# A six-layer cross network on one core: one remainder transposed by VectorE, one group of products moved, one load cut into twelve

## The chip, the cores and the metric

The kernel runs on one NeuronCore of one Trainium2 chip. The metric is the device time of one execution in microseconds (us), as the median of several runs. In what follows PE is TensorE's matmul side and PEld its weight load, DVE is VectorE, ACT is ScalarE, POOL is GpSimd and SP is SyncE; a "q" behind a name (SPq, ACTq) is the part of that engine that issues DMAs and waits.

## The reference

The inputs are x0 of 4096 rows by 416 columns, six weight matrices of 416 by 416 and six biases of 416, all bf16. Six times the current x is multiplied by a matrix, a bias is added, the sum is multiplied element by element by x0, and x is added.

```python
B, F, D, L = 4096, 26, 16, 6
def reference(x0, ws, bs):
    x = x0
    for l in range(ws.shape[0]):
        x = x0 * (x @ ws[l] + bs[l]) + x
    return x
```

## The kernel before

**Layout.** x is kept transposed, with features on the 128 partitions and rows of x0 along the free axis. 416 features are three blocks of 128 (k and m run over them) and a remainder of 32. The three blocks lie in XM: XM[0] holds x0, XM[1] and XM[2] are used in turn for the later layers. The remainder lies in XR in the same way, packed: the 4096 rows are two halves (s = 0, 1) of four column groups of 512 (g = 0 to 3), and the 32 remainder features of group g lie on partitions 32g to 32g+31. XRd is a copy of x0's remainder with the two halves of the partitions exchanged, used by one block of the first layer (m = 1).

**How x0 gets there.** The three blocks come by eight transposing loads on SP's queue (load_x0t, L75), four to a half. The remainder can't come that way. For the first half, four loads on ACT's queue (load_xrem0, L80) bring 64-byte pieces of rows into xrig, four PE transposes (x0_rem, L155) write them to PSUM, and three DVE copies (L158) fill XR[0] and XRd. For the second half, one load on SP's queue (load_xrem1, L84), placed between the transposing loads of that half, fills xrem, a POOL copy (L132) rearranges it into xrig, and x0_rem then does with it as with the first: four PE transposes into half of the PSUM tile pr, and three DVE copies.

**First layer** (first_layer, once for each half). Full products (L212, 128x128 weights, 512 columns), remainder rows (row, L219: 32 partitions of weights, four groups side by side in the array), and products that make the remainder features (mm_rem, L191 and L196: 32 columns of weights, four groups side by side). The outputs of three m and a half-half h lie in PSUM tiles of two banks each; there are four such tiles in all, so a new one waits until ACT has read an old one. ACT adds the bias and moves each tile to SBUF (L163), DVE multiplies by x0 (L164) and adds x (L167). The remainder takes the same way through L171, L172 and L173. For the first half, the call of x0_rem for the second half stands after mm_rem and before the elementwise work of h = 1.

**Layers two to five** (the loop over l from 1). The work is six blocks (s, m), taken in pairs: n = 0, 2, 4 is the first block of a pair. A block is 48 products in column tiles (L179) and four row products (L185). Behind the first pair (n = 0) comes rem_pair: the remainder products of both halves (8 of L191 and 24 of L196) into one PSUM tile, then two ACT and four DVE operations that fill the next XR.

**Last layer.** Rows of the output are made directly, 128 at a time: full products (L325), remainder (L331) and bias (L334), then ACT (L352) and two DVE operations (L353, L342) that multiply by X0rows and add XLrows. X0rows holds x0 by rows and is loaded by four DMAs on SP's queue (L123), behind all weights; bLr (L125) follows. XLrows is x after layer five, put back to rows by transposing DMAs on SP's queue (L203).

**Order.** The order of instructions on each engine follows the program, with a scheduler that may move DVE and ACT work among neighbours; what is handed to keep_in_program_order stays as written. Each engine works its own list in order. DMAs are issued in order on each queue, and a DMA semaphore that is used again makes the issue wait for its earlier user.

Of the kernel before, what the change touches and what calls it, by code (L numbers as in the profile page):

```python
# [11 lines left out]
BF16 = mybir.dt.bfloat16  # L12
# [4 lines left out]
def kernel(  # L17
# [7 lines left out]
    nc = tc.nc  # L25
    B, D = x0.shape
    L = ws.shape[0]
    P = 128
    NK = 3
    R = D - NK * P  # L30
    assert R == 32 and B == 4096 and D == 416 and L >= 2
    NS = 2
    NG = 4
    CW = 512
    SW = NG * CW
    NBT = B // P
# [3 lines left out]
    big = ctx.enter_context(tc.tile_pool(name="big", bufs=1))  # L40
# [4 lines left out]
    x0_v = x0.rearrange("(bt p) d -> p bt d", p=P)  # L45
    out_v = out.rearrange("(bt p) d -> p bt d", p=P)

    ident = const.tile([P, P], BF16)
# [9 lines left out]
    X0rows = big.tile([P, NBT, D], BF16)  # L58
    XLrows = big.tile([P, NBT, D], BF16)
    scrR = [big.tile([P, 4, P], BF16, name=f"scrR{s}") for s in range(NS)]  # L60
    xrem = big.tile([P, 16, R], BF16)
    xrig = big.tile([P, NS, 4, P], BF16)
    XRd = big.tile([P, NS * CW], BF16)
    XM = [big.tile([P, NK, B], BF16, name=f"XM{i}") for i in range(3)]
    XR = [big.tile([P, NS * CW], BF16, name=f"XR{i}") for i in range(3)]

    def col0(s, g):
        return SW * s + CW * g

    def load_wm(eng, l):  # L70
        eng.dma_start(WM[:, l], ws[l, 0:NK * P, :].rearrange("(k p) n -> p k n", p=P))

    def load_x0t(s, g):
        c0 = col0(s, g)
        nc.sync.dma_start_transpose(out=XM[0][:, :, c0:c0 + CW], in_=x0[c0:c0 + CW, 0:NK * P])  # L75

    def load_xrem0():
        with nc.allow_non_contiguous_dma(reason="64B row segments"):
            for i in range(4):
                nc.scalar.dma_start(xrig[:, 0, i, :].rearrange("p (g r) -> p g r", g=NG), x0_v[:, i:16:4, NK * P:D])  # L80

    def load_xrem1():
        with nc.allow_non_contiguous_dma(reason="64B row segments"):
            nc.sync.dma_start(xrem[:], x0_v[:, 16:32, NK * P:D])  # L84

    def load_wr0():
        nc.scalar.dma_start(WR[0:R, 0, :], ws[0, NK * P:D, :])
# [17 lines left out]
    for g in range(1, NG):  # L105
        dst, src = WR[32 * g:32 * g + 32, 0, :], WR[0:R, 0, :]
# [4 lines left out]
    for g in range(2, NG):  # L111
        load_x0t(0, g)
    load_x0t(1, 0)
    load_xrem1()
    for g in range(1, NG):
        load_x0t(1, g)
    load_wm(nc.sync, 1)
# [1 line left out]
        load_wr(nc.sync, g, 1, L)  # L119
    for l in range(2, L):  # L120
        load_wm(nc.sync, l)
    for q in range(4):
        nc.sync.dma_start(X0rows[:, 8 * q:8 * q + 8, :], x0_v[:, 8 * q:8 * q + 8, :])  # L123
    for g in range(NG):
        nc.sync.dma_start(bLr[32 * g:32 * g + 1, :], bs[LL:LL + 1, :])  # L125

    def fill_wd(l0, l1):
        for g in range(NG):
            nc.gpsimd.tensor_copy(WD[32 * g:32 * g + 32, l0:l1, g, :], WR[32 * g:32 * g + 32, l0:l1, NK * P:D])

    fill_wd(0, 1)
    nc.gpsimd.tensor_copy(xrig[:, 1].rearrange("p i (g r) -> p i g r", g=NG), xrem[:].rearrange("p (g i) r -> p i g r", g=NG))  # L132
    fill_wd(1, L)

    wps = psum.tile([P, CW], FP32, tag="ps", name="wps")
# [14 lines left out]
        nc.vector.tensor_copy(bM[:], pb[:, 0:NK, 0:L])  # L150
        nc.vector.tensor_copy(bR[:], pb[:, 3, 0:L])

    def x0_rem(s, tpr):
        for i in range(4):
            nc.tensor.transpose(tpr[:, 128 * i:128 * i + 128], xrig[:, s, i, :], ident[:])  # L155
        for dst, src in ((slice(0, P), slice(0, P)), (slice(64, P), slice(0, 64)), (slice(0, 64), slice(64, P))):
            to = XR[0] if dst == src else XRd
            nc.vector.tensor_copy(to[dst, CW * s:CW * s + CW], tpr[src])  # L158

    def ew_main(l, s, m, h, pt, cur, nxt, pin=False):  # L160
        c0 = col0(s, 2 * h)
        t = tpool.tile([P, 2 * CW], BF16, name="t")
        nc.scalar.activation(t[:], pt[:].rearrange("p a b -> p (a b)"), ACT.Identity, bias=bM[:, m, l:l + 1], scale=1.0)  # L163
        prod = nc.vector.tensor_tensor(out=t[:], in0=t[:], in1=XM[0][:, m, c0:c0 + 2 * CW], op=ALU.mult)  # L164
        if pin:
            tc.keep_in_program_order(prod)
        nc.vector.tensor_tensor(out=nxt[:, m, c0:c0 + 2 * CW], in0=t[:], in1=cur[:, m, c0:c0 + 2 * CW], op=ALU.add)  # L167
# [21 lines left out]
    def mm_rem(l, s, pr, cur, curR):  # L189
        for g in range(NG):  # L190
            nc.tensor.matmul(pr[32 * g:32 * g + 32, :], lhsT=WD[:, l, g, :], rhs=curR[:, CW * s:CW * s + CW],  # L191
                             start=True, stop=False, tile_position=(0, 32 * g))
        for k in range(NK):
            for g in range(NG):
                c0 = col0(s, g)
                nc.tensor.matmul(pr[32 * g:32 * g + 32, :], lhsT=WM[:, l, k, NK * P:D], rhs=cur[:, k, c0:c0 + CW],  # L196
                      start=False, stop=(k == NK - 1), tile_position=(0, 32 * g))

    def new_pts():
        return [psum.tile([P, 2, CW], FP32, tag="ps", name=f"pt{h}") for h in range(2)]  # L200

    def xl_dmat(s, k, nxt):
        nc.sync.dma_start_transpose(out=XLrows[:, 16 * s:16 * s + 16, 128 * k:128 * k + 128],  # L203
                                    in_=nxt[:, k, SW * s:SW * s + SW])

    def first_layer(s):
        cur, curR, nxt, nxtR = XM[0], XR[0], XM[1], XR[1]

        def full(pt, m, h, gl, after_row):
            c0 = col0(s, 2 * h + gl)  # L210
            for k in range(NK):
                nc.tensor.matmul(pt[:, gl, :], lhsT=WM[:, 0, k, 128 * m:128 * m + 128], rhs=cur[:, k, c0:c0 + CW],  # L212
                                 start=(k == 0 and not after_row), stop=(k == NK - 1 and after_row))

        def row(pt, m, h, opens):
            for gl in range(2):
                rg = 32 * ((2 * h + gl) ^ (2 if m == 1 else 0))
                src = XRd if m == 1 else curR
                nc.tensor.matmul(pt[:, gl, :], lhsT=WR[rg:rg + 32, 0, 128 * m:128 * m + 128],  # L219
                                 rhs=src[rg:rg + 32, CW * s:CW * s + CW],  # L220
                                 start=opens, stop=not opens, tile_position=(rg, 0))

        def ph(m):
            return psum.tile([P, 2, CW], FP32, tag="ps", name=f"ph{m}")

        pa = [ph(m) for m in range(NK)]
        if s == 0:
            for m in range(NK):
                full(pa[m], m, 0, 0, False)
            tp0 = psum.tile([P, CW], BF16, tag="ps", name="tpr")  # L230
            x0_rem(0, tp0[:])
            for m in range(NK):
                full(pa[m], m, 0, 1, False)
        else:
            for m in range(NK):
                for gl in range(2):
                    full(pa[m], m, 0, gl, False)
        pb = [ph(0)]
        row(pa[0], 0, 0, False)
        row(pb[0], 0, 1, True)  # L240
        row(pa[2], 2, 0, False)
        row(pa[1], 1, 0, False)
        for m in range(NK):
            ew_main(0, s, m, 0, pa[m], cur, nxt)
        for m in range(NK):
            if m:
                pb.append(ph(m))
            for gl in range(2):
                full(pb[m], m, 1, gl, m == 0)
        row(pb[1], 1, 1, False)  # L250
        row(pb[2], 2, 1, False)
        pr = psum.tile([P, 2, CW], FP32, tag="ps", name="pr")
        mm_rem(0, s, pr[:, 0, :], cur, curR)
        if s == 0:
            x0_rem(1, pr[:, 1, :].bitcast(BF16)[:, 0:CW])
        for m in range(NK):
            ew_main(0, s, m, 1, pb[m], cur, nxt, pin=(s == 0))
        ew_rem(0, s, pr[:, 0, :], curR, nxtR)
# [3 lines left out]
    for s in range(NS):  # L262
        first_layer(s)
# [16 lines left out]
    for l in range(1, LL):  # L280
        nxt, nxtR = XM[1 + (l % 2)], XR[1 + (l % 2)]
        feeds_last = (l == LL - 1)
        tiles = [(s, m) for s in range(NS) for m in range(NK)]
        pts = {}

        def finish(t):
            s, m = t
            for h in range(2):
                ew_main(l, s, m, h, pts[t][h], cur, nxt)
            if feeds_last:  # L290
                xl_dmat(s, m, nxt)

        for n in range(0, len(tiles), 2):
            ta, tb = tiles[n], tiles[n + 1]
            pts[ta] = new_pts()
            for g in range(NG):
                mm_full(l, ta[0], ta[1], g, pts[ta], cur, True, False)
            mm_row(l, ta[0], ta[1], pts[ta], curR, False, True)
            pts[tb] = new_pts()
            mm_row(l, tb[0], tb[1], pts[tb], curR, True, False)  # L300
            if feeds_last and n == 4:
                xl_rem(0)
            finish(ta)
            for g in range(NG):
                mm_full(l, tb[0], tb[1], g, pts[tb], cur, False, True)
            finish(tb)
            if n == 0:
                rem_pair(l, cur, curR, nxtR, feeds_last)
        if feeds_last:
            xl_rem(1)  # L310
        cur, curR = nxt, nxtR

    l = LL
# [97 lines left out]
```

## Time and profile before

| what | value |
|---|---|
| median of 3 runs | 130.45 us (130.38 to 130.53) |
| profiled execution | 130.58 us |
| span of that execution, first to last instruction | 128.8 us |
| granted TensorE clock, mean | 1.000 |
| PE busy | 123.6 us (96%), 1691 matmuls |
| DVE busy | 106.7 us (83%) |
| ACT busy | 86.9 us (67%) |
| POOL busy | 6.2 us (5%) |
| DMA | 16.37 MB |

The span is shorter than the time by what lies before the first and after the last instruction. The groups that the change touches:

```profile
L191 PE MATMUL pr<-XR,WD 128*32 128x512 bf16 x40 | 3.9, 381 | 0.0
L132 POOL COPY xrig<-xrem 128x512 bf16<-128x512 bf16 x1 | 1.1, 1057 | 3.7 <-DMA xrem<-in_x_dram 3.7
L158 DVE COPY XRd<-pr 64x512 bf16<-64x512 bf16 x2 | 0.8, 422 | 0.0
L158 DVE COPY XR<-pr 128x512 bf16<-128x512 bf16 x1 | 0.4, 425 | 0.5 <-PE pr L155 0.5
L155 PE MATMUL pr<-ident,xrig 128*128 128x128 bf16 x4 | 0.4, 222 | 0.0
```

Each line is a group: source line, engine, operation, output and inputs with their shapes, the number of instructions, then the busy time in us and the mean of one in ns, and behind the second bar the idle time of the engine just before them and what ended it. Matmuls are pipelined: a mean of 381 ns does not mean that PE was held that long by each. The time that a group holds PE is read from the chain of waits.

### The profile page before, as it was taken

Reading aid. Unit: us, or ns where it says so; the run is one execution under the profiler, and the core shown is the slowest. Engines: PE = TensorE matmul, PEld = TensorE weight load, DVE = VectorE, ACT = ScalarE, POOL = GpSimd, SP = SyncE. Lnnn points to the kernel's source line nnn. Section 1 sums busy time; section 2 is a strip of 40 time slices with the busy share of each in tenths; the row PEclk is TensorE's granted clock in tenths of the full one; section 3 lists DMA queues with packets and bytes.
Section 4 is the critical chain, followed back from the end, with each engine's and each line's share of the span. In section 5 each row is a group of like instructions: output and inputs, shape, how many; then the busy total and the mean of one; then the engine's idle time right before and its main releaser. Section 6 shows DMA issues by size and latency. Waiting matters only on the chain.

```text
span 128.8 us, 3973 instructions
## 1 busy us (share of the span) xinstructions
PE 123.6 (96%) x1691; PEld 55.1 (43%) x1691; DVE 106.7 (83%) x195; ACT 86.9 (67%) x99; POOL 6.2 (5%) x18
## 2 busy tenths in 40 slices
PE   7999999999999999999999999999999999999960
PEld 3343443344545444434444544444444445445420
DVE  0023989999999898989898989898989899898991
ACT  0138873887848667848668848668858896569670
POOL 4004300600000000000000000000000000000000
PEclk9999999999999999999999999999999999999999
DMA  4999999999990000000000000000297999985754
GB/s 95 244 231 207 163 153 264 253 328 333 336 291 9 5 0 8 0 0 5 0 5 0 5 0 5 0 5 0 45 163 169 119 237 191 217 261 186 235 178 138
DMA packets 42102, 16.37 MB, mean 127 GB/s; under 512 B 30906, under 2 KB 42084, under 8 KB 42084
## 3 DMA queue, kind: packets, MB, share of 16 engines
q1 hardware_dynamic: 39368, 15.53, 53.9%
q10 hardware_dynamic: 2716, 0.59, 2.5%
q8 instruction: 13, 0.21, 0.7%
q14 instruction: 5, 0.04, 0.1%
HBM read 6.15 MB, written 3.41 MB: 74 GB/s over the span
## 4 chain that ended last, share of the span: by engine, by line
PE 89%; DVE 6%; issue 2%; ACT 1%; DVEq 0%
PE pt L179 49%; PE ph L212 13%; PE py L325 8%; PE pt L185 5%; PE pr L196 5%; PE wps L139 4%; DVE t L353 4%; DVE o L342 2%; PE pr L191 2%; PE ph L219 1%; PE py L331 1%; PE py L334 1%; ACT t L352 1%; PE tpr L155 0%; PE pr L155 0%
## 5 line engine op out<-in xcount | busy, mean ns | idle before, releaser
L179 PE MATMUL pt<-XM,WM 128*32 128x512 bf16 x1152 | 65.2, 379 | 0.0
L163 ACT ACTIVATE t<-pt,bM 128x1024 bf16<-128x1024 f32 x48 | 49.6, 1115 | 18.5 <-PE pt L185 18.5
L164 DVE TENSOR_TENSOR t<-t,XM 128x1024 bf16<-128x1024 bf16 x60 | 41.4, 690 | 5.2 <-ACT t L163 5.2
L167 DVE TENSOR_TENSOR XM<-t,XM 128x1024 bf16<-128x1024 bf16 x60 | 41.8, 697 | 3.4
L179 PEld LDWEIGHTS <-WM 128*32 128x32 bf16 x1152 | 29.7, 97 | 33.8 <-issue 5.1
L352 ACT CAST t<-py 128x416 bf16<-128x416 f32 (+1 forms) x23 | 14.8, 642 | 4.8 <-PE py L325 2.6
L325 PE MATMUL py<-WM,XM 128*128 128x416 bf16 x96 | 17.7, 340 | 0.0
L212 PE MATMUL ph<-XM,WM 128*128 128x512 bf16 x72 | 16.5, 381 | 0.0
L163 ACT ACTIVATE t<-ph,bM 128x1024 bf16<-128x1024 f32 x12 | 12.5, 1114 | 3.4 <-PE ph L219 3.4
L325 PEld LDWEIGHTS <-XM 128*128 128x128 bf16 x96 | 9.0, 98 | 8.5 <-issue 1.4
L353 DVE TENSOR_TENSOR t<-t,X0rows 128x416 bf16<-128x416 bf16 (+1 forms) x23 | 10.4, 457 | 1.2 <-ACT t L352 1.2
L342 DVE TENSOR_TENSOR o<-t,XLrows 128x416 bf16<-128x416 bf16 (+1 forms) x23 | 10.4, 456 | 0.0
L212 PEld LDWEIGHTS <-WM 128*128 128x128 bf16 x72 | 6.7, 98 | 8.4 <-issue 1.1
L171 ACT ACTIVATE t<-pr,bR 128x512 bf16<-128x512 f32 x10 | 6.4, 685 | 2.7 <-PE pr L196 2.1
L196 PE MATMUL pr<-XM,WM 128*32 128x512 bf16 x120 | 8.2, 379 | 0.0
L185 PE MATMUL pt<-XR,WR 32*128 32x512 bf16 x96 | 7.3, 379 | 0.0
L139 PE MATMUL wps<-const-bfloat16-1.0 128*128 128x512 bf16 (+1 forms) x12 | 4.9, 592 | 0.8 <-PEq L395 0.8
L104 ACT ACT_TABLE_LOAD x1 | 1.3, 1283 | 6.0 <-DMA XM<-in_x_dram 6.0
L173 DVE TENSOR_TENSOR XR<-t,XR 128x512 bf16<-128x512 bf16 x10 | 4.2, 425 | 0.7
L196 PEld LDWEIGHTS <-WM 128*32 128x32 bf16 x120 | 3.2, 97 | 3.0
L150 DVE CAST bM<-pb 128x18 f32<-128x18 bf16 x1 | 0.2, 177 | 5.1 <-PE pb L149 5.1
L172 DVE TENSOR_TENSOR t<-t,XR 128x512 bf16<-128x512 bf16 x10 | 4.2, 420 | 0.0
(38 smaller groups left out, 33.5 us busy)
## 6 DMA issues: line engine op xcount, KB each, us to landing
X0rows<-in_x_dram SPq DMA_DIRECT2D x4, 832.0 KB, 11.5
out_dram<-o SPq DMA_DIRECT2D x9, 208.0 KB, 2.5
WM<-in_ws_dram SPq DMA_DIRECT2D x5, 312.0 KB
out_dram<-o SPq DMA_DIRECT2D x13, 104.0 KB, 1.9
WR<-in_ws_dram SPq DMA_DIRECT2D x4, 130.0 KB, 4.1
WM<-in_ws_dram ACTq DMA_DIRECT2D x1, 312.0 KB
XM<-in_x_dram SPq DMA_TRANSPOSE x8, 4.9
xrig<-in_x_dram ACTq DMA_DIRECT2D x4, 32.0 KB, 4.2
```

Source lines behind the costliest of these rows:

```text
L139: nc.tensor.matmul(wps[:, 0:cols], lhsT=warm[:, 0:P], rhs=warm[:, 0:cols], start=True, stop=True)
L163: nc.scalar.activation(t[:], pt[:].rearrange("p a b -> p (a b)"), ACT.Identity, bias=bM[:, m, l:l + 1], scale=1.0)
L164: prod = nc.vector.tensor_tensor(out=t[:], in0=t[:], in1=XM[0][:, m, c0:c0 + 2 * CW], op=ALU.mult)
L167: nc.vector.tensor_tensor(out=nxt[:, m, c0:c0 + 2 * CW], in0=t[:], in1=cur[:, m, c0:c0 + 2 * CW], op=ALU.add)
L179: nc.tensor.matmul(pts[g // 2][32 * q:32 * q + 32, g % 2, :], lhsT=WM[:, l, k, 128 * m + 32 * q:128 * m + 32 * q + 32], rhs=cur[:, k, c0:c ...
L185: nc.tensor.matmul(pts[g // 2][:, g % 2, :], lhsT=WR[32 * g:32 * g + 32, l, 128 * m:128 * m + 128], rhs=curR[32 * g:32 * g + 32, CW * s:CW ...
L196: nc.tensor.matmul(pr[32 * g:32 * g + 32, :], lhsT=WM[:, l, k, NK * P:D], rhs=cur[:, k, c0:c0 + CW], start=False, stop=(k == NK - 1), tile ...
L212: nc.tensor.matmul(pt[:, gl, :], lhsT=WM[:, 0, k, 128 * m:128 * m + 128], rhs=cur[:, k, c0:c0 + CW], start=(k == 0 and not after_row), sto ...
L325: nc.tensor.matmul(py[:, 0:D], lhsT=cur[:, k, q_cols(q, g)], rhs=WM[:, l, k, :], start=((not closes) and k == 0), stop=(closes and k == NK ...
L342: tc.keep_in_program_order(nc.vector.tensor_tensor(out=o, in0=t, in1=xl, op=ALU.add))
L352: nc.scalar.copy(tv, src)
L353: tc.keep_in_program_order(nc.vector.tensor_tensor(out=tv, in0=tv, in1=X0rows[:, b, :], op=ALU.mult))
```

## The change

Three things are changed together.

- The remainder of x0's second half is loaded in another arrangement (16 consecutive rows to a partition instead of one row of each block of 128), on ACT's queue instead of SP's; a memset of one column of xrem by DVE, placed behind the first half's copies, makes the load wait for it. DVE transposes it in blocks of 32x32 straight into XR[0], and copies the two exchanged halves from there into XRd. The four PE transposes, the POOL copy and the second half of xrig are gone. These DVE operations and the ACT issue are held in program order.
- rem_pair of layer two (l = 1) is called behind the second pair of blocks (n = 2) instead of the first. The later layers keep it at n = 0.
- X0rows is loaded by twelve DMAs of two or three blocks of 128 rows, instead of four of eight.

```diff
-    xrig = big.tile([P, NS, 4, P], BF16)
+    xrig = big.tile([P, 4, P], BF16)
...
+    def pin(ins):
+        tc.keep_in_program_order(ins)
...
     def load_xrem1():
+        pin(nc.vector.memset(xrem[:, 0, 0:1], 0.0))
         with nc.allow_non_contiguous_dma(reason="64B row segments"):
-            nc.sync.dma_start(xrem[:], x0_v[:, 16:32, NK * P:D])
+            pin(nc.scalar.dma_start(xrem[:], x0[SW:2 * SW, NK * P:D].rearrange("(p t) r -> p t r", p=P)))
...
     load_x0t(1, 0)
-    load_xrem1()
     for g in range(1, NG):
         load_x0t(1, g)
...
-    for q in range(4):
-        nc.sync.dma_start(X0rows[:, 8 * q:8 * q + 8, :], x0_v[:, 8 * q:8 * q + 8, :])
+    for q in range(12):
+        b0, b1 = NBT * q // 12, NBT * (q + 1) // 12
+        nc.sync.dma_start(X0rows[:, b0:b1, :], x0_v[:, b0:b1, :])
...
     fill_wd(0, 1)
-    nc.gpsimd.tensor_copy(xrig[:, 1].rearrange("p i (g r) -> p i g r", g=NG), xrem[:].rearrange("p (g i) r -> p i g r", g=NG))
     fill_wd(1, L)
...
-    def x0_rem(s, tpr):
+    def x0_rem0(tpr):
         for i in range(4):
-            nc.tensor.transpose(tpr[:, 128 * i:128 * i + 128], xrig[:, s, i, :], ident[:])
+            nc.tensor.transpose(tpr[:, 128 * i:128 * i + 128], xrig[:, i, :], ident[:])
         for dst, src in ((slice(0, P), slice(0, P)), (slice(64, P), slice(0, 64)), (slice(0, 64), slice(64, P))):
             to = XR[0] if dst == src else XRd
-            nc.vector.tensor_copy(to[dst, CW * s:CW * s + CW], tpr[src])
+            pin(nc.vector.tensor_copy(to[dst, 0:CW], tpr[src]))
+        load_xrem1()
+
+    def x0_rem1():
+        pin(nc.vector.transpose(XR[0][:, CW:2 * CW].rearrange("p (j t) -> p t j", t=16), xrem[:]))
+        for dst, src in ((slice(64, P), slice(0, 64)), (slice(0, 64), slice(64, P))):
+            pin(nc.vector.tensor_copy(XRd[dst, CW:2 * CW], XR[0][src, CW:2 * CW]))
...
-            x0_rem(0, tp0[:])
+            x0_rem0(tp0[:])
...
         if s == 0:
-            x0_rem(1, pr[:, 1, :].bitcast(BF16)[:, 0:CW])
+            x0_rem1()
...
-            if n == 0:
+            if n == (2 if l == 1 else 0):
                 rem_pair(l, cur, curR, nxtR, feeds_last)
```

More of the change, by code (lines that the diff above doesn't have):

```diff
@@ L79, in load_xrem0 @@
             for i in range(4):
-                nc.scalar.dma_start(xrig[:, 0, i, :].rearrange("p (g r) -> p g r", g=NG), x0_v[:, i:16:4, NK * P:D])
+                nc.scalar.dma_start(xrig[:, i, :].rearrange("p (g r) -> p g r", g=NG), x0_v[:, i:16:4, NK * P:D])
     def load_xrem1():
+        pin(nc.vector.memset(xrem[:, 0, 0:1], 0.0))
         with nc.allow_non_contiguous_dma(reason="64B row segments"):
-            nc.sync.dma_start(xrem[:], x0_v[:, 16:32, NK * P:D])
+            pin(nc.scalar.dma_start(xrem[:], x0[SW:2 * SW, NK * P:D].rearrange("(p t) r -> p t r", p=P)))
     def load_wr0():
```

## The prediction

> **What bounds the kernel now.** I read the page's busy line first, then the chain of waits, first by engine and then in order of time, then the timeline of the first layer, where the change puts most of its edits.
>
> ```profile
> PE 123.6 (96%) x1691; PEld 55.1 (43%) x1691; DVE 106.7 (83%) x195; ACT 86.9 (67%) x99; POOL 6.2 (5%) x18
> ...
> PEclk9999999999999999999999999999999999999999
> ...
> PE 89%; DVE 6%; issue 2%; ACT 1%; DVEq 0%
> ```
>
> A busy PE proves little, but the chain does: it runs on PE for 89% of the span, at a granted clock of 9 tenths or more throughout. In order of time:
>
> ```profile
> 15.73 0.33 PE pr L191 x4
> 16.06 0.65 PE pr L196 x12
> 16.71 0.33 PE pr L155 x4
> 17.04 3.88 PE ph L212 x18
> 20.93 0.54 PE ph L219 x8
> 21.47 3.99 PE ph L212 x18
> 25.46 0.33 PE ph L219 x4
> ...
> 29.90 2.71 PE pt L179 x48
> 32.60 0.21 PE pr L191 x4
> 32.82 0.65 PE pr L196 x12
> 33.47 0.22 PE pr L191 x4
> 33.68 0.65 PE pr L196 x12
> 34.33 2.59 PE pt L179 x48
> 36.92 0.54 PE pt L185 x8
> ```
>
> The columns are start, time on the chain, and what ran. From 5.62 to 115.45 us it has no entry of another engine, and its only break is at 8.40, where a first-half transpose waits for an xrig load. So any PE time removed before 115 moves the end, and any PE wait added there is paid in full; nothing done for DVE, ACT, POOL or a queue gains by itself. Behind 115.45 the chain is ACT and DVE work that starts when PE releases it; DVE sits idle 0.42 us for ACT before its L353 at 116.55, so it can follow a PE that is up to 0.42 us earlier.
>
> The covers that matter are these rows of the timeline (start, length, engine, line, operation; in brackets the idle time before it):
>
> ```profile
> 9.66 1.10 ACT L108 COPY WR<-WR 32x416 bf16<-32x416 bf16 x2 [2.07 <-DMA WR<-in_ws_dram]
> ...
> 10.31 0.58 SPq L84 DMA_DIRECT2D xrem<-in_x_dram  x1
> ...
> 11.09 4.13 ACT L163 ACTIVATE t<-ph,bM 128x1024 bf16<-128x1024 f32 x4 [0.33 <-PE ph L219]
> 11.35 3.57 PEld L212 LDWEIGHTS <-WM 128*128 128x128 bf16 x18 [0.42 <-issue]
> 11.35 4.06 PE L212 MATMUL ph<-XM,WM 128*128 128x512 bf16 x18
> ...
> 15.62 0.98 DVE L167 TENSOR_TENSOR XM<-t,XM 128x1024 bf16<-128x1024 bf16 x1
> ```
>
> **The change part by part.**
>
> *Transposes off PE.* The four transposes L155 of the second half (0.33 us on the chain) go. They were full-array work between the column-tiled remainder products (L196, 128*32) and full products (L212). The chain shows a price for such a switch: 18 L212 matmuls behind the transposes take 3.88 us, the same 18 behind the row-tiled L219 take 3.99; L191 costs 0.33 where it follows L219 and 0.21 where it follows another column-tiled group. A switch thus costs about 0.11 us. Four transposes back to back start 0.056 us apart, which makes 0.22, and 0.33 less 0.22 is again 0.11. That switch remains, and now falls on the L212 group. So the saving is (0.33 + 3.88) - 3.99 = 0.22 us, not 0.33. Bounds: 0.22 if the switch stays, 0.33 if it goes with the transposes. I take 0.22, since both other kinds of change of tile show the price.
>
> The Trainium skill, TensorEngine Tiling (Array Packing), section Key Properties, says that changing the tiling mode, not just the tile, drains TensorE. The 0.11 us of these rows agrees; without that rule the sum would be 0.33.
>
> *POOL.* The copy L132 (1.06 us) goes; nobody on the chain waited for POOL but L155. Beside it, the DVE add at 15.62 took 0.98 us where its group's mean is 0.70, so DVE may gain 0.28, hidden.
>
> *DVE.* Three copies from PSUM (0.42 + 0.86 = 1.28 us, 17.08 to 18.40) become one 32x32 transpose of 128x512 and two copies SBUF to SBUF of 64x512, plus a memset (L93's took 0.06). The trace has no such transpose. Nearest rows: 0.42 for 512 elements (L158), 0.69 for 1024 (L164), 1.06 for POOL's rearranging copy of the same tile. I take 0.69, with 0.42 and 1.06 as ends; the copies at most 0.42 each as now. That is 1.53 (1.26 to 1.90) against 1.28. It starts when the first three pairs end (16.60; ACT's delay of 0.3, below, and the 0.28 from POOL cancel) instead of at 17.08, so it ends at 18.1 (17.9 to 18.5); the product behind it started at 18.31. PE wants this half's XR at the row products, at 20.86 before and 20.6 now. Some 2 us of cover; if the chain slipped past 20.6, PE would pay each us beyond.
>
> The Trainium skill, VectorE: DVE Perf Modes, section The three transpose paths, gives 311 ns for a 128x128 bf16 transpose on VectorE; four of these, an estimate, are 1.24 us, which would end the block at 18.7. No run before shows it, and the sum stays.
>
> *xrem's load moves from SP's queue to ACT's.* On SP it took 0.58 us of issue between two x0 transposes, so the three later transposes, and all loads behind them, issue up to 0.6 us sooner. On ACT it stands between L108 and the first L163 and waits for the memset, behind the copies that end at 9.99; L108 ends at 10.76, so the wait is over by then. Behind it in ACT's order are all the L163 activations, and the second group of ph waits for the first to free its PSUM tile. Issue time: 0.37 to 0.66 for one xrig load on ACT, 0.585 for this very load on SP, 0.74 for the shortest X0rows load. I take 0.585. ACT is then free near 11.37 instead of 10.76, and the first L163 starts at about 11.4 instead of 11.09. It ends at 12.51 (1.11 each) and PE needs the tile at 12.65 (11.35 and six products of 0.22). The cover is 0.28 us of ACT's wait plus 0.44 between 12.21 and 12.65: any issue up to about 0.7 us is free, and each 0.1 beyond costs 0.1. Below: nothing gained, since PE does not wait here. The data land 4.6 us after issue on SP: 10.8 + 4.6 = 15.4, before DVE wants them at 16.6. While DVE waits for them its h=1 products queue behind, and PE only from 20.6 on.
>
> *Layer two's remainder products.* 32 matmuls (0.21 + 0.65 + 0.22 + 0.65 = 1.73 us), two L171 (1.27) and four DVE operations of 0.42 move behind the fourth block. Both old and new place are between column-tiled products, so no switch is added: 0 on PE. Blocks three and four come 1.73 us sooner. Block three needs block one's PSUM tiles: four L163 from 29.72 end at 33.85, the first two at 31.8, and PE arrives at 32.4; the second pair is wanted at 35.0. Block four needs the second half of XM, last written at 30.53 + 0.69 = 31.2, by about 35. The new XR is wanted by layer three's row products at 48.4; products at 38.2 to 39.9 give it by about 43. All covered; at 32.4 the margin is 0.6. Layers three and four run a block pair without remainder after one with it, with the same 5.29 per 96 products.
>
> *X0rows in twelve loads.* Eight more issues on SP (0.74 us each at the least, 6 us); the four took 7.84 us up to 31.12 and SP has nothing of weight behind them but bLr until its transposes at 91.49, and X0rows is read from 107.4. The bytes are the same. Cost 0; lower bound 0, since nobody waited for them.
>
> Sum: -0.22 us on PE, all else covered. The profiled execution was 130.58 us, its span 128.8, so 1.78 lie around it; the span becomes 128.58 and that execution 130.36. The median of the runs, 130.45, becomes 130.23. A difference of 0.2%, 0.26 us, is about what a measurement of this kernel can tell from no change, so the forecast is just inside it.
>
> **Rivals.**
>
> *A. The switch goes with the transposes, or DVE's relief adds a little.* Then the gain is 0.33 or slightly more: 130.1. For it: no row shows column tiles followed directly by L212. Against: 0.11 appears at each other switch.
>
> *B. ACT's issue is longer than its cover (slower).* One mechanism: xrem's 2048 pieces of 64 bytes hold ACT, the first L163 is late, its PSUM tile comes free after 12.65, and PE stands before the second ph. It decides from 0.7 us of issue; it beats the saving from 0.93. The first WM load on SP had 1.41 us of issue, although with a wait perhaps in it; at 1.41 PE would lose 0.7, and the time is 130.45 - 0.22 + 0.7 = 130.9. For it: the margin is only 0.14 us at my value. Against: the same load took 0.585 on SP, and four times a quarter of it on ACT never over 0.66 each.
>
> *C. xrem lands late.* On its own queue it shares engines with x0's transposes; only a landing after some 19 us, against my 15.4, holds PE's row products. At 20 it costs 1 us: 131.2. Against: a landing of 9 us would be twice any of the first 15 us (4.2 to 6.4).
>
> *D. The gain doesn't reach the end,* because DVE's tail does not follow: 130.45. Against: DVE's 0.42 us idle before 116.55.
>
> **How the numbers follow.** Forecast 0.42, A 0.27, B 0.14, C 0.07, D 0.10. Faster by over 0.2%: nearly all of A and a quarter of the forecast, which lies 0.04 us from the border (0.10), less some of A that stays inside: 0.35. Same: the rest of the forecast, D and a little of B: 0.46. Slower: most of B, and C: 0.19. The range runs from 130.0 (A and a tenth for the spread of the runs) to 130.75 (B up to an issue of 1.2 us): it leaves out C and the worst of B. The forecast's own range is 130.1 to 130.35.
>
> **What would show it.** Right: no transposes on PE between L196 and the second half's full products, that first group of 18 at 3.99 on the chain, PE without waits up to the tail, and the span at 128.6. Wrong: the group at 3.88 (A); an idle PE before the second ph at 12.65 and an ACT issue of over 0.7 us (B); DVE waiting for xrem beyond 17 us and PE before the second half's row products (C); PE earlier but a last DVE add that is not (D). A PE wait at 32.4 or 35 would show the move of the remainder products costing something that I put at nothing.

## The result and the profile after

The changed kernel took 130.26 us (median of 16 runs, 130.2 to 130.73), the kernel before beside it 130.5 us (16 runs). The ratio is 0.998 with a 95% interval of 0.9973 to 0.9988: faster by 0.2%, about 0.24 us, and by the interval between 0.16 and 0.35 us. The profiled execution took 130.33 us, its span is 128.5.

The chain of waits of the changed kernel, in order of time (start, time on the chain, what ran; the remainder's lines L191 and L196 are now L200 and L205, L212 is L221, L219 is L228, L179 is L188):

```profile
8.65 2.10 PE ph L221 x9
10.74 0.65 PE ph L228 x8
11.39 3.99 PE ph L221 x18
15.38 0.33 PE ph L228 x4
15.71 0.33 PE pr L200 x4
16.04 0.65 PE pr L205 x12
16.69 3.99 PE ph L221 x18
20.68 0.54 PE ph L228 x8
...
38.19 0.22 PE pr L200 x4
38.41 0.65 PE pr L205 x12
39.06 0.22 PE pr L200 x4
39.27 0.65 PE pr L205 x12
```

There are no transposes between L205 and the 18 products at 16.69, and these take 3.99 where they took 3.88. From L196/L205 to the row products of the second half it was 0.33 + 3.88 and is 3.99: 0.22 less. The remainder products of layer two take 1.74 at 38.19 and took 1.73 at 32.60. Layers three to five keep their length: their first blocks behind the remainder products start at 53.32, 72.56 and 91.79, before at 53.57, 72.80 and 92.04, and PE begins the last layer at 103.47, before at 103.71.

The timeline where the load and the DVE transpose are:

```profile
9.95 0.06 DVE L86 MEMSET xrem<- 128x1 bf16 x1
10.05 0.64 ACTq L88 DMA_DIRECT2D xrem<-in_x_dram  x1
10.20 0.54 ACT L112 COPY WR<-WR 32x416 bf16<-32x416 bf16 x1
...
11.11 4.13 ACT L172 ACTIVATE t<-ph,bM 128x1024 bf16<-128x1024 f32 x4 [0.37 <-PE ph L228]
...
15.64 0.69 DVE L176 TENSOR_TENSOR XM<-t,XM 128x1024 bf16<-128x1024 bf16 x1
...
16.25 2.35 DVE L165 STREAM_TRANSPOSE XR<-xrem 128x512 bf16<-128x512 bf16 x1
...
18.64 0.61 DVE L167 COPY XRd<-XR 64x512 bf16<-64x512 bf16 x2
```

The load's issue (0.64 us) stands behind the copy L112 in ACT's list, yet it ran beside it. The first L172 starts at 11.11, before it was 11.09. And the DVE transpose takes 2.35 us; it starts without a wait for xrem.

### The profile page after: what moved, and what is told of

Read it like the earlier page. It is cut to its first block, busy times and chain, and to the rows that moved or that the text cites. A ratio compares the mean times of both kernels' runs of the same rounds, so it can differ in the third digit from the quotient of the medians.

```text
span 128.5 us, 3976 instructions
## 1 busy us (share of the span) xinstructions
PE 122.4 (95%) x1687; PEld 54.8 (43%) x1687; DVE 108.1 (84%) x196; ACT 86.8 (67%) x99; POOL 4.5 (4%) x17
## 4 chain that ended last, share of the span: by engine, by line
PE 83%; DVE 6%; DMA 4%; ACTq 2%; issue 2%; ACT 1%; DVEq 0%
PE pt L188 49%; PE ph L221 11%; PE py L334 8%; PE pt L194 5%; PE pr L205 5%; DMA xrig<-in_x_dram 4%; DVE t L362 4%; DVE o L351 2%; PE pr L200 2%; PE ph L228 1%; PE py L340 1%; ACTq L83 1%; PE py L343 1%; ACT t L361 1%; ACTq L104 1%
## 5 line engine op out<-in xcount | busy, mean ns | idle before, releaser
L188 PE MATMUL pt<-XM,WM 128*32 128x512 bf16 x1152 | 65.2, 379 | 0.0
L172 ACT ACTIVATE t<-pt,bM 128x1024 bf16<-128x1024 f32 x48 | 49.6, 1115 | 18.2 <-PE pt L194 18.2
L188 PEld LDWEIGHTS <-WM 128*32 128x32 bf16 x1152 | 29.7, 97 | 33.8 <-issue 5.1
L221 PE MATMUL ph<-XM,WM 128*128 128x512 bf16 x72 | 16.4, 379 | 0.7 <-DMA XM<-in_x_dram 0.7
L172 ACT ACTIVATE t<-ph,bM 128x1024 bf16<-128x1024 f32 x12 | 12.5, 1114 | 3.9 <-PE ph L228 3.9
L221 PEld LDWEIGHTS <-WM 128*128 128x128 bf16 x72 | 6.8, 98 | 9.4 <-issue 2.0
L205 PE MATMUL pr<-XM,WM 128*32 128x512 bf16 x120 | 8.2, 379 | 0.0
L194 PE MATMUL pt<-XR,WR 32*128 32x512 bf16 x96 | 7.3, 379 | 0.0
L182 DVE TENSOR_TENSOR XR<-t,XR 128x512 bf16<-128x512 bf16 x10 | 4.4, 435 | 0.6
L142 PE MATMUL wps<-const-bfloat16-1.0 128*128 128x512 bf16 (+1 forms) x12 | 4.0, 505 | 0.8 <-PEq L404 0.8
L205 PEld LDWEIGHTS <-WM 128*32 128x32 bf16 x120 | 3.2, 97 | 3.0
L200 PE MATMUL pr<-XR,WD 128*32 128x512 bf16 x40 | 3.9, 381 | 0.0
```

Of the source, the lines that this page charges most:

```text
L188: nc.tensor.matmul(pts[g // 2][32 * q:32 * q + 32, g % 2, :], lhsT=WM[:, l, k, 128 * m + 32 * q:128 * m + 32 * q + 32], rhs=cur[:, k, c0:c ...
L194: nc.tensor.matmul(pts[g // 2][:, g % 2, :], lhsT=WR[32 * g:32 * g + 32, l, 128 * m:128 * m + 128], rhs=curR[32 * g:32 * g + 32, CW * s:CW ...
```

## The experiments

All times are compared with the kernel before, run beside them on the same chip. The single parts and col_tiles share one chip, the pairs, after_again and two_transposes a second, the others a third. Before the single results, one reading that they need. PE's second group of first-layer products (8.65 above) starts when the loads ahead of it have landed; in 12 of the 14 profiles the last wait before it is for an xrig load, on which the first half's transposes wait. Its start differed from one profiled execution to the next, from 8.55 to 8.98, and from 8.65 to 8.81 between the two profiles of the changed kernel. So besides the medians I give the stretch from that start to the end of DVE's last operation, both from the chain of one profiled execution. It was 117.55 us before (8.63 to 126.18) and 117.29 after (8.65 to 125.94); the second profile of the changed kernel gave 117.37, so 0.08 of a difference can be chance.

### Each part alone

DVE transpose and load alone (dve_alone): the changed kernel with

```diff
-    for q in range(12):
-        b0, b1 = NBT * q // 12, NBT * (q + 1) // 12
-        nc.sync.dma_start(X0rows[:, b0:b1, :], x0_v[:, b0:b1, :])
+    for q in range(4):
+        nc.sync.dma_start(X0rows[:, 8 * q:8 * q + 8, :], x0_v[:, 8 * q:8 * q + 8, :])
...
-            if n == (2 if l == 1 else 0):
+            if n == 0:
```

> The DVE transpose and the load on ACT's queue alone: layer two's remainder products back behind the first pair, X0rows back to four loads. Theory (the whole gain is the PE time of four transposes less the switch that stays): 0.22 to 0.25 us below the kernel before, as the full change, about 130.26; on PE the second half's first group takes 3.99 on the chain. Rival (the other two parts pay, or cover a cost of the first): the transpose took 2.36 us in the changed kernel and the second half's XR was written at 32.96 there, while the remainder products in the old place want it at 33.2; if the margin of 0.2 us is not there, PE waits before L200 at about 33 and the time is 130.35 to 130.5.

The kernel before with the move only (move_alone) and with the twelve loads only (loads_alone):

> The kernel before with only layer two's remainder products moved behind the fourth block. Theory: no change, within 0.1 us of the kernel before, since both places lie between column-tiled products and PE does not wait in either. Rival (the move itself shortens PE or relieves DVE on the path): 0.1 to 0.25 us below it.

> The kernel before with only X0rows in twelve loads. Theory: no change, within 0.1 us of the kernel before, since nothing waits for these loads. Rival (shorter loads help other DMAs, such as instruction fetches): 0.1 to 0.25 us below it.

| kernel | median us | ratio, 95% interval | stretch us |
|---|---|---|---|
| before, beside these | 130.63 | | 117.55 (first profile) |
| dve_alone | 130.69 | 1.0009 (0.9995 to 1.0022) | 117.32 |
| move_alone | 130.55 | 0.9997 (0.9985 to 1.0008) | 117.58 |
| loads_alone | 130.58 | 0.9995 (0.9985 to 1.0006) | 117.53 |

The move and the loads do nothing alone, as expected. The transpose alone is a miss: in its profile PE saves what it should (the products that start at 16.78 last 3.99 to the next group, the stretch is 0.23 shorter than before), but the median does not fall, and not one of its 12 runs was under 130.42. Its profiled execution, 130.61 us, shows where the 0.23 went: the second group started 0.08 later than before, and from the end of DVE's last operation to the end of the execution it is 4.58 us, where the 13 other profiles have 4.38 to 4.42. What made that end longer, and whether the other runs lost their time there too, is not known. So I put the parts together in pairs, beside the changed kernel again.

### The transpose with one other part

dve_move is the changed kernel with the first hunk of the diff above (four loads), dve_loads with the second (remainder products behind the first pair).

> The changed kernel itself, beside the two next ones on one chip. Theory (the gain is the PE time of the transposes): ratio to the kernel before 0.998 as when it was first measured, about 0.22 to 0.25 us. Rival (the first result lay at the lucky end of a spread that the tail makes): a ratio nearer to 1, as the DVE transpose alone showed.

> The changed kernel with X0rows back in four loads. Theory (the twelve loads do nothing): the same time as the changed kernel within 0.1 us. Rival (the twelve loads keep the gain of the transposes from being lost): the time of the kernel before, as with the DVE transpose alone.

> The changed kernel with layer two's remainder products back behind the first pair of blocks. Theory (the move costs and gains nothing): the same time as the changed kernel within 0.1 us. Rival (the move covers the 2.36 us transpose): in the old place XR comes too late in many executions, and the time is that of the kernel before or above, as with the DVE transpose alone.

| kernel | median (lowest) us | ratio, 95% interval | stretch us |
|---|---|---|---|
| before, beside these | 130.59 (130.44) | | |
| after_again | 130.35 (130.24) | 0.998 (0.997 to 0.9989) | 117.37 |
| dve_move | 130.47 (130.23) | 0.9992 (0.9979 to 1.0006) | 117.40 |
| dve_loads | 130.44 (130.23) | 0.9986 (0.9974 to 0.9998) | 117.45 |

The gain of the full change is confirmed. Both pairs reach the same lowest time as the changed kernel, so neither of the other parts is needed for that; their medians lie between, and the interval of dve_move holds 1. dve_alone has neither part, and its lowest time was 130.42; but it ran on another chip and was not repeated, so the loss is not shown to come from the two parts missing together. For dve_loads the chain shows why the place of the remainder products can matter:

```profile
32.34 0.22 PE pr L200 x4
32.55 0.65 PE pr L205 x12
33.20 0.38 PE pr L200 x4
33.58 0.65 PE pr L205 x12
```

And its timeline on DVE:

```profile
16.48 2.36 DVE L165 STREAM_TRANSPOSE XR<-xrem 128x512 bf16<-128x512 bf16 x1 [0.18 <-DMA xrem<-in_x_dram]
...
32.71 0.42 DVE L182 TENSOR_TENSOR XR<-t,XR 128x512 bf16<-128x512 bf16 x1
```

The second L200 takes 0.38 instead of 0.22: PE waits 0.16 us for XR of the second half, which DVE finished at 33.13 (L182 at 32.71, 0.42 long). In the kernel before it was finished at 31.55 and wanted at 33.47. So at the old place the DVE transpose can cost PE time, and the move, worth nothing alone, takes that away. The long transpose is not the whole cause: DVE had waited 0.18 us for xrem first and had no pause from there to L182, so without that wait XR would have been there at 32.95 and PE's wait would have been about nothing. dve_alone had the same order, and in its profiled execution XR was ready at 33.01 and PE, which came at 33.31, did not wait. For the four loads against twelve no profile shows PE waiting, and the intervals overlap. Whether the twelve loads do anything beside the transpose stays open.

### What a transpose costs PE, and what the switch costs

twelve_pe puts twelve transposes back where four were, into the unused half of pr:

```diff
         if s == 0:
+            tpx = pr[:, 1, :].bitcast(BF16)
+            for i in range(12):
+                nc.tensor.transpose(tpx[:, 128 * (i % 4):128 * (i % 4) + 128], xrig[:, i % 4, :], ident[:])
             x0_rem1()
```

> The changed kernel with twelve PE transposes, whose results nobody reads, at the place where four were taken out. Theory (a transpose costs PE 0.056 us, and the switch of tiling 0.11 us is paid there anyway): 0.67 us above the changed kernel, near 130.9 to 131.0; on the chain 0.78 for the twelve with the switch, and the group behind them 3.88. Rival (each transpose costs a quarter of the 0.33 us that the chain showed): 1.0 us above, near 131.3.

131.03 us against 130.35 for after_again (0.68 more; the kernel before was 130.59 beside both). Its chain:

```profile
16.32 0.65 PE pr L205 x12
16.97 0.78 PE pr L266 x12
17.75 0.22 PE ph L221
...
18.02 3.62 PE ph L221 x16
21.63 0.54 PE ph L228 x8
```

The twelve take 0.78 = 12 x 0.056 + 0.11, and the group behind them 3.88, from 17.75 to 21.63 (one of its 18 records is missing). On the chain that is what was expected, 0.67 us more than the 3.99 of the changed kernel; the stretch, 118.07, is 0.70 and 0.78 longer than the changed kernel's two. That the medians agree to 0.01 us is partly luck: the interval of this run's ratio is 0.0030 wide, some 0.4 us.

col_tiles takes the switch away in the changed kernel, by writing the second half's first group in column tiles:

```diff
-                    full(pa[m], m, 0, gl, False)
+                    c0 = col0(s, gl)
+                    for k in range(NK):
+                        for q in range(4):
+                            nc.tensor.matmul(pa[m][32 * q:32 * q + 32, gl, :],
+                                             lhsT=WM[:, 0, k, 128 * m + 32 * q:128 * m + 32 * q + 32],
+                                             rhs=cur[:, k, c0:c0 + CW], start=(k == 0), stop=False,
+                                             tile_position=(0, 32 * q))
```

> The changed kernel with the 18 full products of the second half's first group written as 72 column-tiled ones of 32 columns, as in layers two to five. Theory (a change of tiling costs PE 0.11 us, and the group behind L205 pays it in the changed kernel): no change of tiling is left there, the group takes 3.88 instead of 3.99 and the time falls by 0.11 us against the changed kernel, 0.33 to 0.36 below the kernel before, about 130.15. Rival (0.11 us is the price of whatever follows the remainder products, or belongs to full-array products): the group takes 3.99 or more and the time stays at 130.26 or rises.

The group took 3.88, as expected. The time did not follow: 130.84 us, ratio 1.0016 (1.0001 to 1.0032), slightly slower than before. Its profiled execution took 130.53 us, near the lowest of its runs, and the stretch is 117.56, 0.27 longer than in the changed kernel. What it lost lies behind the last pair of blocks of layer five, in the timeline of col_tiles:

```profile
95.68 4.07 SPq L287 DMA_TRANSPOSE scrR<-XR  x2
...
100.40 0.62 ACT L291 COPY XLrows<-scrR 128x512 bf16<-128x512 bf16 x1 [1.68 <-DMA scrR<-XR]
...
100.93 4.12 ACT L172 ACTIVATE t<-pt,bM 128x1024 bf16<-128x1024 f32 x4
...
104.76 0.69 PE L346 MATMUL py<-WR,XR 32*128 32x416 bf16 x4
```

ACT stands 1.68 us for a transposing DMA, and the activations queued behind it start 0.5 us after the products are done (L194 at 99.99 and 0.43 more, as at other pairs). The lag reaches the last layer, where four L346 take 0.69 instead of the 0.35 or 0.34 of before. On the chain:

```profile
104.93 0.17 PE py L346 x2
105.10 0.35 PE py L346 x2
```

That is 0.52 where the changed kernel has 0.18 (105.09), so 0.34 us are lost, and PE goes on at 105.10, just behind the end of the fourth of those activations (100.93 and 4.12). Counted from the second group, PE had come to the last layer 0.08 sooner than in the changed kernel (8.56 to 103.30 against 8.65 to 103.47), so this loss makes up the 0.27 of the stretch but for rounding. The median lies further off; that part is not in the profile.

In the kernel before, and in loads_alone (the second pair of lines), ACT had slack at this place:

```profile
99.68 0.62 ACT L276 COPY XLrows<-scrR 128x512 bf16<-128x512 bf16 x1 [0.56 <-DMA scrR<-XR]
100.83 4.13 ACT L163 ACTIVATE t<-pt,bM 128x1024 bf16<-128x1024 f32 x4 [0.53 <-PE pt L185]
...
99.90 0.62 ACT L277 COPY XLrows<-scrR 128x512 bf16<-128x512 bf16 x1 [0.80 <-DMA scrR<-XR]
100.81 4.13 ACT L164 ACTIVATE t<-pt,bM 128x1024 bf16<-128x1024 f32 x4 [0.29 <-PE pt L186]
```

The slack is the second number in brackets: 0.53 before, 0.28 in the changed kernel. The earlier PE need not be the reason, since loads_alone has 0.29 with PE where it was before. Nor does the copy stay in place when PE moves: in twelve_pe PE comes to this pair 0.95 us later than in the changed kernel (L194 at 101.10 against 100.15) and the copy 0.88 later (100.57 against 99.69). What is special to col_tiles is the transfer. Its issue began 1.5 us sooner than in the changed kernel (95.68 against 97.17), and its data came 0.7 us later. Only pool_cols below, the other kernel with these column tiles, shows the same (issue at 95.97, copy at 100.86). Why they go together is open.

### ACT out of the way

pool_rows (the changed kernel) and pool_cols (col_tiles) with the two copies into XLrows on POOL:

```diff
-            nc.scalar.copy(XLrows[:, 16 * s:16 * s + 16, NK * P:D].rearrange("p (g i) r -> p i g r", g=NG),
+            nc.gpsimd.tensor_copy(XLrows[:, 16 * s:16 * s + 16, NK * P:D].rearrange("p (g i) r -> p i g r", g=NG),
```

> The changed kernel with the two copies of the last remainder into XLrows on POOL instead of ACT. Theory (ACT stands in these copies for a transposing DMA near 100 us, and in some executions long enough to hold PSUM tiles and so PE; this makes much of the spread): the fastest executions stay at 130.2, the spread above becomes smaller, and the median falls by 0.05 to 0.1 us against the changed kernel. Rival (POOL's copies slow DVE, or the spread is made elsewhere): the same median and spread, or above.

> The changed kernel with both the column-tiled products in the second half's first group and the copies into XLrows on POOL. Theory (the column tiles save 0.11 us on PE, and lost it near 100 us to ACT's wait of 1.68 us for the transposing DMA): with ACT out of that wait the saving reaches the end: 0.1 us below the changed kernel, 130.1 to 130.2, 0.33 us or more below the kernel before. Rival (the loss has another cause, such as the products themselves or PE's heavier instruction stream): the time stays near 130.8, as with the column tiles alone.

pool_rows: 130.39 us (130.2 to 130.5), ratio 0.9985 (0.9976 to 0.9994). No run was above 130.5, where the changed kernel went to 130.77; but the median did not fall, so that half of the expectation failed. pool_cols: 130.29 us (lowest 130.13), ratio 0.9981 (0.9969 to 0.9992), against 130.84 with ACT in the wait. The transfer is late in it too, and the four L346 are back at 0.34, so that wait is what cost col_tiles its saving in the profile. Its stretch is 117.20, the shortest of all, 0.09 and 0.17 under the two profiles of the changed kernel. Against pool_rows, which lacks only the column tiles and ran beside it, the median is 0.10 lower, near the 0.11 of the chain. It beats the kernel before; against the changed kernel (0.998) and pool_rows the intervals overlap, so whether the 0.11 arrives is not settled.

### The DVE transpose

two_transposes does it twice, dense_transpose once without the spread:

```diff
+        pin(nc.vector.transpose(xtra[:].rearrange("p (j t) -> p t j", t=16), xrem[:]))
         pin(nc.vector.transpose(XR[0][:, CW:2 * CW].rearrange("p (j t) -> p t j", t=16), xrem[:]))
```

```diff
-        pin(nc.vector.transpose(XR[0][:, CW:2 * CW].rearrange("p (j t) -> p t j", t=16), xrem[:]))
+        pin(nc.vector.transpose(XR[0][:, CW:2 * CW].rearrange("p (t j) -> p t j", t=16), xrem[:]))
```

> The changed kernel with the DVE transpose done twice, first into a tile that nobody reads. Theory (the 2.36 us of the first are hidden, and PE wants XR at its row products 20.6 us in, while the copies end at 19.25): the second set of 2.36 us moves the end of the copies to 21.6, PE waits about 1.0 us before L228, and the time rises by about 1.0 us to 131.3. Rival (DVE's work here has more cover than that, because PE waits for none of it directly): under 0.3 us. Second rival (DVE's lag reaches layer two as well): 1.5 to 2.4 us.

> The changed kernel with the DVE transpose writing its blocks one behind the other, not spread with a step of 16 columns; this puts the columns of the second half's remainder in another order, so the output isn't the reference's. Theory (the 2.36 us come from the spread writes): the transpose takes 0.7 to 1.3 us. Rival (a transpose of this form takes that long however it writes): 2.2 us or more. The time stays that of the changed kernel in both cases, since PE does not wait for it.

two_transposes: 130.85 us, 0.5 above the changed kernel beside it (130.35), ratio to before 1.0023 (1.0011 to 1.0034). Its chain leaves PE for DVE at that place:

```profile
15.92 0.69 DVE XM L178
16.61 2.27 DVE xtra L166
18.88 2.18 DVE XR L167
21.06 0.04 issue
21.10 0.71 PE ph L230 x8
21.81 3.99 PE ph L223 x18
```

The row products start 12.17 us after the second group (8.93 here), in the changed kernel 12.03 (8.65 to 20.68), and take 0.71 instead of 0.54: PE loses 0.14 + 0.17 = 0.31 us, not 1.0; the stretch (117.61) is longer by the same 0.32, and what else is in the 0.5 of the medians its profile does not show. Two errors of mine made the difference: the second transpose adds 2.2 us, since the two overlap, and the first row products want XR only, not XRd. So XR, ready at 18.6 with one transpose of 2.36, has about 2 us of cover, and the second transpose uses it up.

Of dense_transpose, the groups by line:

```profile
L165 DVE STREAM_TRANSPOSE XR<-xrem 128x512 bf16<-128x512 bf16 x1 | 0.7, 712 | 0.4 <-DMA xrem<-in_x_dram 0.4
```

712 ns instead of 2355: the spread writes cost 1.64 us. The kernel leaves out the right order of those columns, but does the same work with them. The time is 130.37 us, that of the changed kernel, so the 1.64 us are hidden.

## Why the prediction was right, point by point

- **The bound.** Right for this change: PE's price reached the end. Twelve transposes, with no switch added, lengthened the time by 0.68 where PE's own price is 0.67, and four removed took away 0.24. It is no law: in dve_alone and col_tiles PE's saving did not reach the median.
- **The size of the saving.** Right, 0.22 on the chain. The median's 0.24 is nearer to it than can be claimed, with an interval from 0.16 to 0.35. That the switch of tiling stays and falls on the next group is what kept the term from being 0.33: 3.99 in place of 3.88. Rival A fell with it, and twelve_pe confirms the split into 0.056 apiece and 0.11. The Trainium skill's rule that changing the tiling mode drains TensorE (TensorEngine Tiling (Array Packing), Key Properties) agrees; col_tiles shows the 0.11 vanish when the mode does not change.
- **DVE's transpose.** The step that mis-sized a term: I gave 0.69 with ends 0.42 and 1.06, and it took 2.36. All three rows that I took the ends from write with small steps or on another engine; this one writes one column in 16, and the dense form took 0.71. The two copies took 0.61 together, not 0.84. The sum was 2.96 instead of 1.53, and XRd was ready at 19.25 instead of 18.1. It stayed inside the cover to 20.6, so the time was right in spite of it: the sum held because the cover was large, not because the price was known. The Trainium skill's 311 ns for 128x128 (VectorE: DVE Perf Modes, The three transpose paths) makes an estimate of 1.24 us for this size; the dense form was faster and the spread one slower.
- **ACT's issue.** I let it push the first L163 by 0.3 us, with 0.14 us left. It pushed nothing: the issue of 0.64 us ran beside the copy before it. My sum of issue and copy end to end was wrong, and rival B had less for it than I gave.
- **The move of the remainder products.** Right that it costs nothing, but I saw no use in it. With a transpose of 2.36 us, and 0.18 us of waiting for xrem before it, DVE is late into layer two, and PE waits 0.16 us at the old place in dve_loads. I had priced the parts one by one at the durations that I guessed, and so missed that one covers another.
- **Twelve loads.** Nothing in any profile; alone no change. Beside the transpose it is open.
- **Rivals C and D.** xrem's landing was a second term sized too small. I took 4.6 us from issue to landing, as on SP's queue, and had xrem there at 15.4. In the changed kernel it was there when DVE came at 16.25. But in five other profiles DVE waited for it, 0.18 us in dve_loads and 0.31 to 0.36 in dve_move, pool_rows, pool_cols and dense_transpose, and went on 6.4 to 6.6 us after the start of the issue. No row products of the second half waited for that, so C as I wrote it did not happen; but in dve_loads the delay came out again in layer two. D did not happen: DVE's tail followed. A loss of its kind, a saving of PE that does not arrive, showed in col_tiles at another place, near 100 us, where ACT waits for a DMA.

## What to carry to other kernels

When an instruction leaves a chain in which the engine changes its mode, look at what the next group then pays: the price of the switch may stay, and the saving is the difference of the two stretches, not the length of what was removed. When work is moved to an engine with cover, its price is still needed, since what it makes late may be wanted two stages on; a second edit that looks idle can be the one that holds the cover. And where PE is the bound, look for another engine that waits for a transfer with work for PE queued behind that wait: when the transfer is late, a saving on PE can be lost there.

## What the runs showed of the hardware

- A DVE transpose of 128x512 bf16 in blocks of 32x32 took 0.71 us with blocks written one behind the other and 2.35 to 2.52 us with a step of 16 columns between the elements written (eleven transposes in ten profiled executions; the dense form ran in one). Copies of 64x512 from SBUF took 0.29 us in the mean where the same from PSUM took 0.42.
- A DMA issue of 0.64 us on ACT's queue ran while the copy before it was still at work (10.05 to 10.69 beside 10.20 to 10.74).
- PE's second group of first-layer products started between 8.55 and 8.98 us in 14 profiled executions, with the same loads ahead of it. That is a spread of 0.43 us, more than the change brings, and the two medians of the changed kernel differ by 0.09 (130.26 and 130.35).
- The load of xrem on ACT's queue (128 KB) let DVE go on 6.4 to 6.6 us after the start of its issue in the five profiles in which DVE waited for it. The same amount, arranged otherwise and on SP's queue, landed 4.6 us after its issue before.
